# DeltaNet followed by a hardswish MLP on one core: the triangular problems stored with rows and columns changed over, and the first steps in another order

## The chip, the cores and the metric

The kernel runs on one core of one Trainium2 chip. A core has five engines with a queue of instructions each: TensorE (PE, with its weight loads shown as PEld), VectorE (DVE), ScalarE (ACT), GpSimd (POOL) and SyncE (SP), which here issues most of the DMAs. Each engine takes its instructions strictly in order; an instruction that waits holds up everything behind it on its engine. The metric is the device time of one execution in microseconds. A profiled execution has a span, from its first to its last instruction, and a time of its own, which is a little longer.

## The reference

Two blocks in a row. The first is a delta-rule attention over 768 steps, for 4 batches x 8 heads with heads of 48 elements; the second is an MLP on the 3072 x 384 result.

```python
k_n = k / (np.linalg.norm(k, axis=-1, keepdims=True) + 1e-06)
for t in range(S):                          # S = 768
    y[:, :, t] = einsum('bhd,bhde->bhe', q[:, :, t], state)
    v_old = einsum('bhde,bhd->bhe', state, kt)
    state += bt * einsum('bhd,bhe->bhde', kt, vt - v_old)
x = y.transpose(0, 2, 1, 3).reshape(B * S, H * D)   # 3072 x 384
h = x @ w_in                                        # 384 x 2048
g = h * clip(h + 3, 0, 6) / 6
out = g @ w_out                                     # 2048 x 384
```

q, k, v and beta arrive as float32, the two weight matrices as float64.

## The kernel before, in words

**Chunks.** The 768 steps are cut into 24 chunks of 32. Inside a chunk the recurrence is solved in closed form: with L, the strictly lower triangle of the chunk's scaled k-by-k products, one needs X, the inverse of a unit triangular 32x32 matrix, for each of the 32 pairs of batch and head. The partitions are 4 batches x 32 positions.

**The steps of one chunk t** (names as in the profile). `load_k`, `load_q`, `load_v` issue the DMAs (lines 140 to 175), four per chunk and tensor. `norms` makes 1/|k|: ACT squares (L386), DVE reduces (L392), ACT takes the root (L396), DVE two reciprocals and two small steps (L399 to L410). `mask` (L458) makes beta times the triangle on POOL, `prep` scales k (kb, L480, POOL), turns kb and q on PE (pt, L496), copies them to KQ on ACT (L504), multiplies them on PE (sc, L517) and masks the products on DVE into L (first output of L528) and LB (second). `scaled` (L468) makes beta times k. `chain` carries the state: PE multiplies state and KQ (ks, L776), DVE forms R (L789), PE X times R (pz, L797), ACT copies it to Z (L883), PE makes the update su (L894), which DVE takes from the state (L909); for the output ACT (L813) and DVE (L789) form y from ks, PE makes py (L797), DVE adds it (L832; for chunk 0 ACT copies it, L830), PE turns y (yt, L842) and ACT writes xT (L846).

**The inverses.** Chunk 0 is group 0, then there are six groups of up to four chunks. For chunk 0 `product` builds X out of 32x32 products on PE (pi, L566) with copies and transposes between them (L574 to L626, V by ACT in L594 and L613). For every other group the 128 problems of four chunks are laid on the 128 partitions: `taken` (L448) moves all of L into the tile A by one DVE transpose of 32x32 blocks, so that one partition holds one whole 32x32 matrix; a column-by-column elimination follows, two DVE instructions for each column (L700 and L705 in `halves_of`, L729 and L734 in `inverse`), then a memset of the diagonal (L710, L738), and `given` (L452) moves the result back into X. Group 1 goes by `halves_of`, which solves the two 16x16 halves of every matrix, and `join` (pi, L654, with L661 to L680) puts the halves together chunk by chunk; the others go by `inverse`.

**Weights.** The float64 weights come in 16 pieces of 768 KB (`load_w`, L310). DVE and ACT put together their float32 values: ACT four scale steps for each piece (L335), DVE three (L357, L362, L368).

**The MLP.** `up` multiplies a piece of w_in with xT (ph, L948), ACT and DVE make the activation g (L956, L959), `down` multiplies by w_out (po, L988); from the third block of 256 tokens on, `down_by_seven` makes it from seven products of half size (po, L1053, with DVE sums L1039). Block 0 is made in two halves of 128 tokens, the words `ua` and `ub`.

**What sets the order.** The first part of the program, up to and including the MLP of block 0 and the second group's inverse, is written out in `ORDER`, a list of 804 words (lines 22 to 44). Each word takes one step of a generator: `k`, `q`, `v`, `B`, `w` issue one DMA (k, q, v, beta, weight piece); `z` are settings, one of which turns beta (L234); `s` are POOL's memsets; `n0` to `n9` norms; `m` mask, `p` prep, `b` scaled; `x0` the product for chunk 0, `x1` to `x4` the joins; `i1` and `i2` the inverses of groups 1 and 2; `h` chain, `y` output; `a` ACT's scale steps; `c` DVE's share of the weights; `ua`/`ra`/`ga`, `ub`/`rb`/`gb`, `u`/`ru`/`gu` the MLP's products and its two activation steps; `e` its outputs. The order of the words fixes each engine's queue. Behind `ORDER` a loop over the chunks (L1262) issues the rest in a fixed plan. SP's DMAs share eight completion semaphores with beta's, which ACT issues: each DMA waits for the one eight places before it.

The lines that hold the layout of A:

```python
def problems(A):                                          # L444
    return A.rearrange("p (c i) -> p i c", i=C)
def taken(g, A):
    nc.vector.transpose(out=problems(A), in_=turn(Ls[g]))
def given(g, A):
    nc.vector.transpose(out=turn(inverted(g)), in_=problems(A))
```

`turn` views L or X as 32 positions i times 32 chunk-and-head pairs, a step of 32 elements between neighbours of the innermost axis.

Of the kernel before, what the change touches and what calls it, by code (L numbers as in the profile page):

```python
# [15 lines left out]
ALU = mybir.AluOpType  # L16
# [6 lines left out]
k*3 B k B*3 z n0*3 w z*3 s z q*2 n0 q n0 q v n0 w n0 a p0 a p0 s p0*2 m0 k*2 w p0 a*3 p0 a c a c v  # L23
p0 x0 a c k a x0*4 k a k x0 c k w*2 n1 c a c*2 k a x0 a*2 k a x0 k c*2 x0*2 n1 v c n1 k a q n2 c w
x0 a x0*2 k*2 m1 a*3 n1 s n2 c n1 a*2 x0 n1 c k*2 x0 n1 v x0 b0 n2 p1 c a n2 s b1 q h0 a c*2 h0 c
n2 w n2 a m2 k h0 s n2 q c z k q p1 n4 a y0 a p1 n2*2 p2*2 h0 q a p1 s*2 q*2 n4 p3 w q c n4 p2 c
p1 n4*2 p3 c n4 q*2 n4 b2 c a p2 p3 q*2 p2 p1 a q p2 c q*2 a p2 k p3 a p3 p4*3 q k m3 p4*2 s p1 p3
v p4 c y0 w y0*2 p3 ua m4 p4 ra ua b4 ua i1*6 ra*2 i1 k w ga i1*2 a ga ua ra i1*2 ua ga*2 i1 ra q
ua v ra a ua v i1 ga i1 ra ga ua s q i1*2 ua i1 ga i1 ra*2 ga i1 a i1*3 h1 ua i1 ra ga v ua ra
i1*2 v a ga i1*2 ga ua ra i1*2 ua a ga y1 i1 ua i1 x1 w x2 ra ua x2 x1 x2 ra ga*2 a x1 ra x1 k x1  # L30
ua x3 k x3 c x1 ra h1 y1 c h1*2 v y1 ga y1*2 q x3 c*2 w x3 a*2 y1 ub a v ub c ga h1 c rb*2 ub q rb
x2*2 k gb*2 v h1 ub q gb ub*2 rb c h2 n5 gb rb h2 gb k x2 ub a m5 v rb gb rb ub c gb y2 ub h2 q rb
w ub gb rb v n5 y2 u gb ub x4 a h2 k*2 q rb q n5 k*2 a n5 a k c rb y2 h2 y2 k gb a k n5 a ub gb y2
h2 ub c rb gb h3 rb ub gb v y2 c k q n5 v x3 h3 x3 y3 k*2 w k h3 a h3 b3 n5 u y3 rb x4 y3 a k n5*2
a w gb y3 c ub k n5 y3*2 rb gb c v n5 c u n5 u h3 ru gu a ru n5 a gu p5 h3 n9 x4 v c p5 b5 u p5 u
a*2 q h4 a p6 p5 a p5 x4 u v ru k c u a ru gu y4 n9 b6 x4 m6 v c q h4 k q gu u x4 k y4 p6 p7 u q
k*3 p6 k p7 h4 k n9 a q h4 p8 p7 p5 a c p5 k u n9 k p7 ru gu h4 p6 p7 m7 n9 h4 q b7 q u a c p6 n9
u p8 ru gu u k c k v n9*2 p8 c n9 b8 n9*3 p6 p8 w u n9 p6 c p8 p7 p8 p7 p9 ru m8 u p8 gu u c q ru
# [9 lines left out]
def kernel(  # L48
# [22 lines left out]
    B, H, S, D = q.shape  # L71
    DM, FF = moe_w_in.shape
    C, DP = 32, 64
# [118 lines left out]
    for j, value in enumerate((1.0, -1.0)):  # L192
        m = mask2[:, j, :]
        for b in range(B):
            nc.gpsimd.memset(mask2[rows(b), j, :], value)
            nc.gpsimd.affine_select(
                out=mask2[rows(b), j, :], in_=mask2[rows(b), j, :], pattern=[[1, C]],
# [246 lines left out]
    def problems(A):  # L444
        return A.rearrange("p (c i) -> p i c", i=C)
# [888 lines left out]
```

## Time and profile before

| | |
|---|---|
| three runs | 691.79, 689.22, 691.63 us; median 691.63 |
| the profiled execution | 690.61 us, its span 688.9 us |
| PE busy | 644.7 us, 94% of the span |
| DVE, ACT, POOL busy | 464.3, 239.1, 92.9 us |
| chain that ended last | PE 76%, DVE 14%, DMA 4%, issue 2%, SP's queue 2% |
| L948 (ph) | 1248 records, 270.0 us |
| L448, L452 (the block transposes) | 6 and 6, 2104 and 2081 ns |
| L729, L734 (the elimination) | 150 and 150, 335 and 361 ns |
| L335 (ACT's scale steps) | 56, 940 ns |

Float32 matmuls appear as two records each, so 32 matmuls are 64 records. The granted clock (PEclk) is the share of its full speed that TensorE was allowed. An engine's idle time counts only where that engine, or one that waits for it, carries the end; a row's releaser is the last thing that the waiting instruction had to have.

### The profile page before, as it was taken

The page shows a single profiled execution, that of the slowest core. Times are in us where ns is not written, and L with a number is a line of the kernel's source. Part 1 is how long each engine was busy: PE and PEld are TensorE (multiplying, and loading weights), DVE is VectorE, ACT ScalarE, POOL GpSimd, SP SyncE. Part 2 cuts the span into 40 slices and gives each one's busy share as a digit, 9 for nine tenths or more (in the row PEclk, how much of TensorE's full clock was granted, in tenths as well). Part 3 has the DMA queues.
Part 4 walks back from the last instruction along what each step waited for, and adds up shares of the span by engine and source line. Part 5 has one row for each costly group of instructions (what it writes and reads, how often), then busy time and mean ns, then how long its engine had stood idle before and what let it go on. Part 6 is the DMA issues. An engine that isn't in the chain of part 4 may idle for free.

```text
span 688.9 us, 25309 instructions
## 1 busy us (share of the span) xinstructions
PE 644.7 (94%) x11208; PEld 565.0 (82%) x11208; DVE 464.3 (67%) x1210; ACT 239.1 (35%) x476; POOL 92.9 (13%) x147
## 2 busy tenths in 40 slices
PE   1468799999999999999999999999999999999997
PEld 1357687767678988988988988988988989989997
DVE  4798776799836986845986745985546985445242
ACT  4886378542132232232232232232232132132220
POOL 5063003331501100501100402100000000000000
PEclk9999799999999999999999999999999999999999
DMA  9877026402132030031020030020020020000000
GB/s 236 240 184 183 4 83 134 83 3 58 29 60 46 3 65 9 3 73 33 4 59 14 3 70 2 3 59 2 3 48 2 2 48 2 25 3 1 25 0 24
DMA packets 88494, 33.20 MB, mean 48 GB/s; under 512 B 80160, under 2 KB 83232, under 8 KB 88384
## 3 DMA queue, kind: packets, MB, share of 16 engines
q1 hardware_dynamic: 88128, 31.29, 19.9%
q8 instruction: 88, 1.44, 0.9%
q10 hardware_dynamic: 256, 0.30, 0.2%
q14 instruction: 22, 0.18, 0.1%
HBM read 26.84 MB, written 4.72 MB: 46 GB/s over the span
## 4 chain that ended last, share of the span: by engine, by line
PE 76%; DVE 14%; DMA 4%; issue 2%; SPq 2%; ACT 1%; POOL 0%; DVEq 0%; ACTq 0%
PE ph L948 33%; PE po L1053 21%; PE po L988 5%; PE ks L776 3%; PE pz L797 3%; DVE A L734 3%; PE pt L496 3%; PE su L894 2%; PE py L797 2%; DVE pr L729 2%; DVE g L1039 2%; PE sc L517 2%; DMA vf<-in_v_dram 1%; PE yt L842 1%; DVE R L789 1%
## 5 line engine op out<-in xcount | busy, mean ns | idle before, releaser
L948 PE MATMUL ph<-xT,w_in 128*128 128x256 f32 (+1 forms) x1248 | 270.0, 369 | 4.2 <-DVE g L959 2.9
L948 PEld LDWEIGHTS ph<-xT,w_in 128*128 128x128 f32 x1248 | 220.2, 192 | 33.9 <-DVE g L959 4.7
L956 ACT ACTIVATE g<-ph,halves 128x256 f32<-128x256 f32 (+1 forms) x208 | 94.8, 457 | 201.7 <-PE ph L948 200.9
L959 DVE SCALAR_TENSOR_TENSOR g<-g,ph 128x256 f32<-128x256 f32 (+1 forms) x208 | 81.0, 396 | 106.0 <-ACT g L956 105.8
L1053 PE MATMUL po<-w_out,g 128*128 128x192 f32 x640 | 113.3, 328 | 0.0
L1053 PEld LDWEIGHTS po<-w_out,g 128*128 128x128 f32 x640 | 103.8, 190 | 0.5
L1053 PE MATMUL po<-spare,g 128*128 128x192 f32 x480 | 84.8, 330 | 0.0
L1053 PEld LDWEIGHTS po<-spare,g 128*128 128x128 f32 x480 | 78.1, 190 | 1.8
L1039 DVE TENSOR_TENSOR g<-g 128x256 f32<-128x256 f32 x160 | 65.5, 463 | 0.5 <-PE po L1053 0.5
L734 DVE TENSOR_TENSOR A<-A,pr 128x30 f32<-128x30 f32 (+9 forms) x150 | 54.2, 361 | 3.7
L335 ACT ACTIVATE spare<-spare,places 128x768 uint16<-128x768 uint16 (+1 forms) x56 | 52.5, 940 | 4.1 <-DVE places L252 3.3
L729 DVE TENSOR_TENSOR pr<-A 128x30 f32<-128x30 f32 (+9 forms) x150 | 50.3, 335 | 3.0
L988 PE MATMUL po<-w_out,g 128*128 128x384 f32 x128 | 45.7, 493 | 0.0
L1060 ACT ACTIVATE o<-po 128x192 f32<-128x192 f32 x40 | 13.2, 330 | 88.1 <-PE po L1053 88.1
L480 POOL TENSOR_TENSOR kb<-kf,inv 128x384 f32<-128x384 f32 x24 | 21.6, 900 | 158.4 <-DVE inv L410 73.7
L458 POOL TENSOR_TENSOR mb<-beta_tok,mask 128x256 f32<-128x256 f32 x48 | 34.5, 741 | 47.2 <-DVE LB L528 47.1
L504 ACT ACTIVATE KQ<-pt 128x512 f32<-128x512 f32 x48 | 28.3, 595 | 35.0 <-PE pt L496 34.6
L846 ACT ACTIVATE xT<-yt 128x384 f32<-128x384 f32 x24 | 11.7, 487 | 64.3 <-PE yt L842 64.3
L988 PEld LDWEIGHTS po<-w_out,g 128*128 128x128 f32 x128 | 22.9, 190 | 11.9
L496 PE MATMUL pt<-ident,kb 128*128 128x128 f32 x96 | 16.2, 295 | 14.7 <-POOL kb L480 14.5
L909 DVE TENSOR_TENSOR state<-state,su 128x384 f32<-128x384 f32 x46 | 23.2, 546 | 9.7 <-PE su L894 9.7
L789 DVE SCALAR_TENSOR_TENSOR y<-ks,parity,y 128x192 f32<-128x192 f32 x46 | 17.0, 412 | 17.6 <-ACT y L813 17.6
(109 smaller groups left out, 601.3 us busy)
## 6 DMA issues: line engine op xcount, KB each, us to landing
kf<-in_k_dram SPq DMA_DIRECT2D x96, 48.0 KB, 2.5
qb<-in_q_dram SPq DMA_DIRECT2D x96, 48.0 KB, 2.3
vf<-in_v_dram SPq DMA_DIRECT2D x96, 48.0 KB, 2.1
out_dram<-o SPq DMA_DIRECT2D x92, 48.0 KB, 1.6
spare<-in_moe_w_in_dram SPq DMA_DIRECT2D x4, 768.0 KB, 5.9
w_out<-in_moe_w_in_dram SPq DMA_DIRECT2D x4, 768.0 KB, 5.8
w_out<-in_moe_w_out_dram SPq DMA_DIRECT2D x4, 768.0 KB, 5.8
spare<-in_moe_w_out_dram SPq DMA_DIRECT2D x4, 768.0 KB, 4.6
```

Of the source, the lines that this page charges most:

```text
L335: nc.scalar.activation(out=z, in_=z if n else d.bitcast(I16)[:, :, :, 3], func=func, bias=places[:, n : n + 1], scale=scale,)
L458: nc.gpsimd.tensor_tensor(out=mb[:, e], in0=beta_tok[:, t, e:H:2].unsqueeze(2).unsqueeze(3).to_broadcast([P, NP, 2, C]), in1=mask2[:].unsq ...
L496: nc.tensor.transpose(pt[:, p, :], src[:, 2 * p : 2 * p + 2].rearrange("p e w -> p (e w)"), ident[:])
L729: nc.vector.tensor_tensor(out=pv, in0=A[:, j, j + 1 :].unsqueeze(1).to_broadcast([n, j, w]), in1=A[:, 0:j, j].unsqueeze(2).to_broadcast([n ...
L734: nc.vector.tensor_tensor(out=A[:, 0:j, j + 1 :], in0=A[:, 0:j, j + 1 :], in1=pv, op=ALU.subtract)
L797: nc.tensor.matmul(ps[rows(place(b)), D * h : D * h + D], lhsT=m(h)[rows(b)], rhs=z[rows(b), D * h : D * h + D], start=True, stop=True, sk ...
L948: nc.tensor.matmul(ph[:, cols], lhsT=w_in[:, s, f * 128 : (f + 1) * 128], rhs=xT[:, s, cols], start=(s == 0), stop=(s == NKT - 1),)
L956: nc.scalar.activation(out=g, in_=ph, func=ACTF.Relu, bias=half, scale=1.0 / 6.0)
L959: nc.vector.scalar_tensor_tensor(out=g, in0=g, scalar=1.0, in1=ph, op0=ALU.min, op1=ALU.mult)
L988: nc.tensor.matmul(pos[c][:], lhsT=gs[blk, f // 2][:, f % 2, c * P : (c + 1) * P], rhs=w_out[:, f, :], start=(f == 0), stop=(f == NFC - 1),)
L1039: nc.vector.tensor_tensor(out=A(f, *out), in0=A(f, *a), in1=A(f, *b), op=op)
L1053: nc.tensor.matmul(ps[n][:], lhsT=A(f - f % 2, *a)[:, f % 2], rhs=b[:, f], start=(f == 0), stop=(f == HF - 1),)
```

## The change

A is stored as the transposed matrix: what was at place (c, i) is at (i, c). `problems` then is the tile in its plain order, the out side of L448 and the in side of L452 run without a step, and the elimination's products and subtractions take rows for columns, in `halves_of` and in `inverse`. The same numbers are computed by the same number of instructions of the same sizes.

`ORDER` is written anew. It holds the same 804 words, each as often as before, in another order. Its first line before and after:

```diff
-k*3 B k B*3 z n0*3 w z*3 s z q*2 n0 q n0 q v n0 w n0 a p0 a p0 s p0*2 m0 k*2 w p0 a*3 p0 a c a c v
+k z k*2 B*2 k B*2 z n0*3 z*2 n0 z m0 n0*3 w s z s a q*2 c a p0 m1 p0 k c k a q*2 p0 w p0 s p0 a*3
...
     def problems(A):
-        return A.rearrange("p (c i) -> p i c", i=C)
+        return A.rearrange("p (i c) -> p i c", c=C)
...
-        D2 = D2.rearrange("p k (c i) -> p k c i", i=C)
+        D2 = D2.rearrange("p k (i c) -> p k i c", c=C)
...
-            pv = pr[0:n, 0 : 2 * j * w].rearrange("p (k c i) -> p k c i", k=2, c=j)
+            pv = pr[0:n, 0 : 2 * j * w].rearrange("p (k i c) -> p k i c", k=2, c=j)
...
-                out=pv, in0=D2[:, :, j, j + 1 : HC].unsqueeze(2).to_broadcast([n, 2, j, w]),
-                in1=D2[:, :, 0:j, j].unsqueeze(3).to_broadcast([n, 2, j, w]), op=ALU.mult,
+                out=pv, in0=D2[:, :, j + 1 : HC, j].unsqueeze(3).to_broadcast([n, 2, w, j]),
+                in1=D2[:, :, j, 0:j].unsqueeze(2).to_broadcast([n, 2, w, j]), op=ALU.mult,
...
-                out=D2[:, :, 0:j, j + 1 : HC], in0=D2[:, :, 0:j, j + 1 : HC], in1=pv,
+                out=D2[:, :, j + 1 : HC, 0:j], in0=D2[:, :, j + 1 : HC, 0:j], in1=pv,
...
-                out=pv, in0=A[:, j, j + 1 :].unsqueeze(1).to_broadcast([n, j, w]),
-                in1=A[:, 0:j, j].unsqueeze(2).to_broadcast([n, j, w]), op=ALU.mult,
+                out=pv, in0=A[:, j + 1 :, j].unsqueeze(2).to_broadcast([n, w, j]),
+                in1=A[:, j, 0:j].unsqueeze(1).to_broadcast([n, w, j]), op=ALU.mult,
...
-                out=A[:, 0:j, j + 1 :], in0=A[:, 0:j, j + 1 :], in1=pv, op=ALU.subtract
+                out=A[:, j + 1 :, 0:j], in0=A[:, j + 1 :, 0:j], in1=pv, op=ALU.subtract
```

The queues that follow from the new words, for the first chunks. SP: the four pieces of the first k and the first weight piece as before, then half of the first q, half of the second k, the rest of q, the second weight piece, the rest of the second k. DVE: beta's transpose (L234) ahead of the first norm's reduction (L392) instead of behind it, the parity memsets (L255, L258) behind the first norm instead of behind six weight pieces. POOL: the first chunk's mask ahead of its kb. ACT: three scale steps before the first KQ and five after the second, then L594, instead of two and seven. PE: the second chunk's kb and q are turned among and behind the first chunk's products; ahead of the first join stand 24 matmuls ph, ks and 15 ph instead of 27, ks and 18; then the joins follow singly, and in chunk 1's chain su stands ahead of py and yt instead of behind them. From about 170 us of the profiled execution to the end PE, and DVE from the second group's L452 on, have the same queue in both.

## The prediction

> **What bounds the kernel now.** I read the page first: how busy each engine is, and where.
>
> ```profile
> PE 644.7 (94%) x11208; PEld 565.0 (82%) x11208; DVE 464.3 (67%) x1210; ACT 239.1 (35%) x476; POOL 92.9 (13%) x147
> ...
> PE   1468799999999999999999999999999999999997
> PEclk9999799999999999999999999999999999999999
> ```
>
> TensorE (PE) is the bound from about 85 us to the end; the missing tenths stand in the first five of 40 slices. Next I asked for the busy times by stage: stage, its length, then busy time of PE, PEld, DVE, ACT, POOL, the granted clock and the DMA share.
>
> ```profile
> 20.00:30.00 10.00, 4.08 (x192) 3.63 (x192) 8.33 (x14) 8.40 (x13) 0.00 (x0) 1.00 0.91 226
> 30.00:40.00 10.00, 5.76 (x254) 5.07 (x256) 8.08 (x17) 9.74 (x15) 4.67 (x8) 1.00 0.70 150
> 40.00:50.00 10.00, 7.31 (x239) 5.83 (x227) 9.61 (x29) 9.25 (x15) 4.18 (x6) 1.00 0.74 204
> ...
> 70.00:80.00 10.00, 6.80 (x321) 5.83 (x313) 6.00 (x15) 3.00 (x6) 0.00 (x0) 0.66 0.02 5
> ...
> 120.00:130.00 10.00, 10.00 (x230) 7.80 (x230) 7.05 (x17) 6.96 (x14) 3.59 (x5) 1.00 0.43 96
> ...
> 200.00:240.00 40.00, 40.00 (x754) 36.08 (x753) 29.12 (x76) 12.43 (x27) 6.13 (x8) 1.00 0.19 35
> ```
>
> Up to 50 us ACT is nearly full and PE waits; from 200 us PE has 40.0 of 40.0 us. From the moment at which PE is full, the rest is a fixed quantity of matmul work, and both versions issue that work in the same order. So what the head (0 to 55 us) and the join of the first group (55 to 110 us) save, the end receives whole, and nothing else can give much. Third, the instructions of PE and DVE in order of time (start, length, what, idle before it and who ended it):
>
> ```profile
> 55.19 2.94 PE L948 MATMUL ph<-xT,w_in 128*128 128x128 f32 x24 [0.58 <-ACT xT L846]
> 69.54 1.39 PE L654 MATMUL pi<-X,VY 16*32 16x16 f32 x128 [1.85 <-DVE VY L664]
> 74.06 1.65 PE L948 MATMUL ph<-xT,w_in 128*128 128x128 f32 x6
> 92.37 0.94 PE L948 MATMUL ph<-xT,w_in 128*128 128x128 f32 x6
> ```
>
> ```profile
> 8.49 0.98 DVE L234 STREAM_TRANSPOSE beta_tok<-spare 128x768 f32<-128x768 f32 x1 [2.02 <-DMA qb<-in_q_dram]
> 9.39 0.33 DVE L237 TENSOR_REDUCE eye<-ident 128x32 f32<-128x128 f32 x1
> 9.86 0.25 DVE L245 TENSOR_REDUCE corner<-ident 128x16 f32<-128x64 f32 x1
> 54.95 2.10 DVE L448 STREAM_TRANSPOSE A<-L 128x1024 f32<-128x1024 f32 x1
> 66.92 2.09 DVE L452 STREAM_TRANSPOSE X<-A 128x1024 f32<-128x1024 f32 x1
> ```
>
> The MLP's first matmuls (ph) start at 55.19, behind xT. The first group's inverse starts its transpose at 54.95 and frees the join's matmuls (pi) at 69.54. The same six ph records take 1.65 us at 74 us and 0.94 at 92: the granted clock is 0.66 in that stage, 0.50 between 72 and 76.
>
> The sum is made against the profiled execution: 690.61 us, a span of 688.9 and 1.71 around it. It lies 1.02 below the median of the three runs, 691.63.
>
> **Part 1, the layout.** Each group makes one transpose into A (L448) and one out of it (L452), 12 in all at 2.10 and 2.08 us. Before, A is stepped by 32 elements in both, and so are L and X; after, the A side runs without a step and the L or X side still steps. A transpose without any step costs 0.98 us for 768 elements and 0.446 for 256: 0.53 us per 512 elements, so 0.98 + 0.27 = 1.25 us for 1024. Each changed transpose therefore lies between 1.25 and 2.1. Which side is dear? Two reductions read with a step of 32: 64 elements take 0.25 us (L245), 128 take 0.33 (L237), 1.25 ns an element against 1.04 without a step, so a stepped read is nearly free and the stepped write must make the 2.1. L448 then goes to 1.25 and L452 stays: 6 x 0.85 = 5.1 us of DVE time. I take that; the ends are 0 and 12 x 0.85 = 10.2. The products and subtractions between them (L700, L705, L729, L734) change rows for columns. They already run every shape from few long rows to many short ones, and 198 elements cost 0.37 us as 9 rows of 22 and 0.36 as 22 rows of 9: zero, and this is the row itself, not cover.
>
> On the path lies only the first group's pair (54.95 and 66.92, both in the chain) and a little of the second's (139.34): **-0.85**, ends 0 and -1.7, and **-0.3** for the second, ends 0 and -1.3 (all PE idle time from 140 to 180 us is 0.58 + 0.76). The later groups are hidden by PE at 40.0 of 40.0.
>
> The Trainium skill's page "SBUF — State Buffer", section Specifications, says that every access which crosses to a new 16-byte line pays. By that a stepped read pays too and both transposes could stay near 2.1; the first group's term would be 0 and the forecast 0.85 higher. The two reductions speak against it.
>
> **Part 2, the first weight piece.** Its DMA stands fifth on SP's queue in both versions, behind the four pieces of the first k, and waits for nothing in both; the four beta DMAs go by ACT's queue. Zero. What does move on SP: two of the second chunk's k pieces go ahead of half of q, v's first piece goes back behind the next chunks' k, and the second weight piece waits for the first to land (8.61 instead of 6.20 us). Each SP DMA waits for the one eight before it, so I walked the issue times: pieces 2 to 8 go out at about 8.6, 10.5, 12, 16.5, 17.6, 26.5 and 27.5, against 6.2, 9.5, 12.5, 13, 18.4, 23.9 and 30.3. With 5.8 to 5.9 us to land, all are there before ACT comes to them (third piece: lands by about 17, read at 19.8).
>
> **Part 3, the order of the first steps.** DVE now transposes beta (8.49 to 9.47) before it reduces the first k norm (was 5.92), so root, two reciprocals and kb move back by 0.5 us; POOL makes the first mask ahead of kb, which DVE then doesn't wait for. From there ACT is the queue to follow. Before, ACT runs seven scale steps (L335, 0.945 us each) between the second KQ and the copy of the first product (L594, at 21.00); after, five, so L594 comes at about 19.5 and the second product starts at 20.4 instead of 21.90. Following ACT's new queue with the old durations, from the end of its second KQ: 29 scale steps 27.4, 4 squares 1.64, 3 roots 0.75, 8 KQ 4.0, two V copies 0.6, Z and y 0.9: 35.3 us. That begins at about 14.8 and ends with y at 50.1, against 53.40. Before, the same walk has 36.2 us of work from 14.57 and 2.6 us of waits (1.50 at 28.74 for DVE, 0.60, 0.86, 0.26). In the new queue the tight places have slack: V's second copy 0.65 us, the second root 0.8, Z about 0. The last sc waits for the last KQ (49.7), yt ends near 51.2, ph starts near 51.7: -3.5. If the new order has 2.6 us of waits too, it is -0.9. I take **-3.0**, nearer the walk, for Z's missing slack. PE does the same matmuls up to there in both, so this is a plain shift.
>
> In the join PE gets 13 column blocks of ph (0.73 us each) ahead of its first pi instead of 15, then only the first chunk's pi, its pz, and su ahead of py. Counted from the start of ph, the inverse takes as long as before (28 steps and 10 instead of 11 g). PE's idle times before, in order: 0.65, 1.85, 0.93, 0.98, 0.61, 0.68, 0.58, 0.58 = 6.9 us. After, with old transposes: 0.8 where ph waits for g (DVE takes the third g after seven pairs, not five), 2.6 until the first pi, 0.9 until the second, 0.6 for R (queued behind L357 on DVE), 0.6 for Z, 0.6 for y, 0.7 for the next pz, 0.58 twice: 8.0. So +1.1. Against it stands the slow clock: two ph (1.65 and 1.49 against 0.94), pz (1.50 against 0.88), pi (1.29 against 0.73) and su (1.20 against 0.89) lost 2.7 us before; with state updated some 14 us sooner and ph work left to fill in, I take that half of it stays: -1.35. Ends: +1.1 and -1.6; sum **-0.25**. The moved parity memsets (0.44 us of DVE) go into DVE's wait for sc (3.19 us before), zero; without that wait they would cost their 0.44.
>
> The page "TensorE: Matmul & The Clock Gate", section "What's actually happening", has the half clock after an idle window of about 3.4 us. Here 0.50 followed 68 to 72 us, in which PE was busy 1.5 of 4 us, with no single gap above 1.85. By the page alone my gaps of at most 2.6 us would leave the clock full and the sum 1.35 lower; the row says that a sparse stretch is enough.
>
> **Sum.** -0.85 - 0.3 - 3.0 - 0.25 = -4.4 on 690.61: 686.2. Half of the distance to the median added: **686.7 us**.
>
> **Rivals.** (a) The transposes stay at 2.1, the step on either side being enough: L452 at 2.08 against L448 at 2.10 doesn't tell the sides apart. -3.25: 687.9. (b) The head's gain is eaten: ACT keeps its 2.6 us of waits (-0.9) and the join costs +1.1 at the old clock, -0.85 and -0.3 remain: about -1, 690.2. For it speaks that ACT's slack is under 1 us at four places. (c) Slower: the join is sparse enough to hold the clock at half for long. At half clock 1.65 us do the work of 0.94, so 10 us of it lose 4.3; before it held for some 9 us between 70 and 84. To turn the forecast's -4.4 into +3.5 takes 7.9 us, 18 further microseconds of it; 25 give +10.8 - 4.4 and 697. Against it: after 85 us PE has no gap above 0.58, and the clock came back within 4 us of dense ph work.
>
> **Numbers.** What a measurement of this kernel tells from no change is 0.5%, 3.5 us: faster is below 688.2, slower above 695.1. Forecast 0.53, of which 0.50 faster and 0.03 same; (a) 0.15, at the border, 0.09 faster and 0.06 same; (b) 0.18, same; (c) 0.14, slower. So 0.59, 0.27 and 0.14. Low end: -3.5 - 1.7 - 1.3 - 1.6 = -8.1 with a run as fast as the profiled one, 682. High end: (b) and the milder half of (c), 694.5. The forecast's own range is 684 to 689.
>
> **What would show it.** Right: L448 near 1.25 and L452 near 2.08; L594 near 19.5; y near 50; the first ph near 51.7; state's second update near 71 instead of 84; PE idle from 55 on about 7 us. Wrong: an ACT wait of more than 1 us between 15 and 50 (a weight piece or a product late); L448 still 2.1; a granted clock below 0.7 for more than 10 us after 60; or PE idle time after 140 us, which would mean that DVE, not PE, had become the bound.

## The result, and the profile after

The changed kernel takes 693.45 us (median of 20 executions, 690.22 to 696.64); before takes 691.32 us (20 executions, 689.22 to 695.41). The ratio is 1.0028, with a 95% interval of 1.0010 to 1.0045: slower by some 2 us, within the 0.5% that the forecast called the same, and 6.8 us above the forecast of 686.7. In a second set of runs the ratio was 1.0033 (1.0014 to 1.0051).

The profiled execution after took 690.50 us with a span of 688.8, next to 690.61 and 688.9 before. It is one of the quickest of the 20, so it flatters the change by about 3 us; the medians carry the verdict, the profile shows the places.

First the page of the changed kernel: the busy times, PE in 40 slices, and the granted clock.

```profile
PE 646.2 (94%) x11208; PEld 567.6 (82%) x11208; DVE 465.5 (68%) x1210; ACT 239.6 (35%) x476; POOL 96.1 (14%) x147
...
PE   1677899999899999999999999999999999999997
...
PEclk9989899999999999999999999999999999999999
```

The second and third slice of PE have risen from 4 and 6 to 6 and 7; the fourth has fallen from 8 to 7. And PE is 1.5 us longer busy with the same matmuls, and the clock has a dip in the third slice that before had not. The same stages as in the prediction (stage, its length, busy times of PE, PEld, DVE, ACT, POOL, granted clock, DMA share, GB/s):

```profile
20.00:30.00 10.00, 5.80 (x256) 5.39 (x256) 8.89 (x19) 9.84 (x14) 0.91 (x1) 1.00 0.87 215
30.00:40.00 10.00, 6.22 (x227) 4.83 (x222) 9.45 (x19) 9.84 (x16) 4.43 (x6) 0.97 0.87 209
40.00:50.00 10.00, 8.27 (x252) 7.26 (x252) 8.67 (x15) 8.97 (x14) 6.83 (x9) 0.69 0.77 189
70.00:80.00 10.00, 8.17 (x317) 7.24 (x313) 6.04 (x14) 5.37 (x9) 0.00 (x0) 0.66 0.13 23
...
200.00:240.00 40.00, 40.00 (x753) 36.08 (x752) 29.12 (x76) 12.45 (x27) 6.15 (x8) 1.00 0.20 36
```

ACT is fuller up to 40 us (9.84 of 10 against 8.40 and 9.74): the new order does pack it. From 200 us on nothing has changed. Now PE in order of time (start, length, what, idle before it and who ended it), first before and then after; the counts are of records, two to a matmul:

```profile
37.26 1.17 PE L797 MATMUL pz<-vf,X 32*32 32x48 f32 x44 [0.98 <-issue]
...
47.39 0.99 PE L517 MATMUL sc<-KQ 64*32 64x64 f32 x68 [0.64 <-issue]
...
180.27 0.86 PE L517 MATMUL sc<-KQ 64*32 64x64 f32 x64 [1.03 <-ACT y L813]
```

```profile
37.65 0.35 PE L797 MATMUL py<-Z,LB 32*32 32x48 f32 x10
39.90 1.33 PE L797 MATMUL py<-Z,LB 32*32 32x48 f32 x54 [1.90 <-issue]
...
48.04 0.71 PE L517 MATMUL sc<-KQ 64*32 64x64 f32 x46 [0.47 <-ACT KQ L504]
50.49 1.04 PE L517 MATMUL sc<-KQ 64*32 64x64 f32 x82 [1.74 <-issue]
...
52.59 2.94 PE L948 MATMUL ph<-xT,w_in 128*128 128x128 f32 x24 [0.58 <-ACT xT L846]
...
66.06 0.73 PE L654 MATMUL pi<-X,VY 16*32 16x16 f32 x64 [1.19 <-DVE VY L664]
...
180.39 0.86 PE L517 MATMUL sc<-KQ 64*32 64x64 f32 x64 [1.78 <-ACT y L813]
```

The first ph starts 2.6 us sooner than before, at 52.59. The first two lines to look at are those that end in "issue": in the middle of a run of equal small matmuls, after the 10th py and after the 46th sc, PE stands still for 1.90 and 1.74 us and waits for no engine and no data that the profile shows. Before has two such pauses ahead of ph, of 0.98 and 0.64 us. The last sc stands straight ahead of yt and ph. What fed it was early, as ACT's line for y shows. Below it are DVE's block transposes of the first group and of the second:

```profile
19.18 0.36 ACT L594 ACTIVATE VY<-pi 128x256 f32<-128x256 f32 x1
...
48.84 0.50 ACT L830 ACTIVATE y<-py 128x384 f32<-128x384 f32 x1
```

```profile
8.29 0.98 DVE L234 STREAM_TRANSPOSE beta_tok<-spare 128x768 f32<-128x768 f32 x1 [6.24 <-DMA qb<-in_q_dram]
...
52.35 1.97 DVE L448 STREAM_TRANSPOSE A<-L 128x1024 f32<-128x1024 f32 x1
63.57 1.96 DVE L452 STREAM_TRANSPOSE X<-A 128x1024 f32<-128x1024 f32 x1
...
137.61 1.98 DVE L448 STREAM_TRANSPOSE A<-L 128x1024 f32<-128x1024 f32 x1
170.68 1.95 DVE L452 STREAM_TRANSPOSE X<-A 128x1024 f32<-128x1024 f32 x1
```

The second group's pair before:

```profile
139.34 2.12 DVE L448 STREAM_TRANSPOSE A<-L 128x1024 f32<-128x1024 f32 x1
170.41 2.07 DVE L452 STREAM_TRANSPOSE X<-A 128x1024 f32<-128x1024 f32 x1
```

y starts 4.1 us sooner than before (52.92), ph only 2.6. And the transposes cost 1.97 and 1.96 us: the layout has brought 0.13 us each, not 0.85.

Where do the 2.6 us go? PE's idle time from the first ph to the ks of chunk 5 (at about 171 us) is 8.55 us against 7.57, summed over the stages between; its busy time for nearly the same work is 0.9 longer; some 0.8 us of lead are left at 171, and between 177 and 181 us, where PE waits for y (1.78 us against 1.03), they go too. From there to the end the two profiles run 0.1 us apart. DVE's rows tell where y is held up: the second group's transpose into A starts 1.7 us sooner than before (137.61 against 139.34), the one out of it 0.3 later (170.68 against 170.41). Two microseconds of lead are lost between the two.

### The profile page after: what moved, and what is told of

It is laid out like the page before. It is cut to its first block, busy times and chain, and to the rows that moved or that the text cites. A ratio compares the mean times of both kernels' runs of the same rounds, so it can differ in the third digit from the quotient of the medians.

```text
span 688.8 us, 25313 instructions
## 1 busy us (share of the span) xinstructions
PE 646.2 (94%) x11208; PEld 567.6 (82%) x11208; DVE 465.5 (68%) x1210; ACT 239.6 (35%) x476; POOL 96.1 (14%) x147
## 3 DMA queue, kind: packets, MB, share of 16 engines
q8 instruction: 88, 1.44, 0.9%
## 4 chain that ended last, share of the span: by engine, by line
PE 73%; DVE 14%; DMA 4%; issue 4%; ACT 3%; SPq 1%; POOL 0%; DVEq 0%; POOLq 0%; ACTq 0%
PE ph L948 33%; PE po L1053 21%; PE po L988 4%; PE py L797 3%; PE ks L776 3%; DVE A L734 3%; PE pz L797 2%; DVE pr L729 2%; PE su L894 2%; DVE g L1039 2%; PE sc L517 2%; PE pt L496 2%; ACT spare L335 2%; DMA kf<-in_k_dram 1%; DVE R L789 1%
## 5 line engine op out<-in xcount | busy, mean ns | idle before, releaser
L734 DVE TENSOR_TENSOR A<-A,pr 128x30 f32<-128x30 f32 (+9 forms) x150 | 54.6, 364 | 3.6
L729 DVE TENSOR_TENSOR pr<-A 128x30 f32<-128x30 f32 (+9 forms) x150 | 50.5, 337 | 3.0
L480 POOL TENSOR_TENSOR kb<-kf,inv 128x384 f32<-128x384 f32 x24 | 23.0, 965 | 156.0 <-issue 69.7
L776 PEld LDWEIGHTS ks<-state,KQ 64*64 64x64 f32 x1472 | 23.8, 134 | 7.7 <-issue 6.9
```

Of the source, the lines that this page charges most:

```text
L729: nc.vector.tensor_tensor(out=pv, in0=A[:, j + 1 :, j].unsqueeze(2).to_broadcast([n, w, j]), in1=A[:, j, 0:j].unsqueeze(1).to_broadcast([n ...
L734: nc.vector.tensor_tensor(out=A[:, j + 1 :, 0:j], in0=A[:, j + 1 :, 0:j], in1=pv, op=ALU.subtract)
L776: nc.tensor.matmul(ph[y][c, e, D * p : D * p + D], lhsT=KQ[r, p * B // 2 + b // 2, 2 * y : 2 * y + 2, :].rearrange("k y c -> k (y c)"), rh ...
```

## Experiments

Medians are in us; ratios are to the runs of before on the same chip, with their 95% intervals. "New head" is the first 225 words of `ORDER` as changed (to the first matmul of ph), "new rest" all that follows; where a head and a rest of different origin are joined, the rest's words keep their order and those that the head has already taken are left out.

### Which part of the change costs: the layout or the order

```diff
 e1:  problems(), halves_of(), inverse() as changed; ORDER as before
 e2:  ORDER as changed; problems(), halves_of(), inverse() as before
 e3:  the changed kernel
```

> The new layout with the old order of the steps. Theory: the layout is worth almost nothing and costs nothing. A transpose falls from 2.10 to 1.97 us, about 0.13 us each, two of them on the path of the first group: 691 us, ratio to before 0.998 to 1.001, granted clock as before (0.990). Rival (the layout is what costs, since rows and columns of the elimination steps are changed over): ratio 1.002 to 1.004, and the elimination steps L729 and L734 dearer than 335 and 361 ns.

> The new order of the steps with the old layout. Theory: the order makes the whole of the result. It starts ph some 2.5 us sooner, and gives that back in the join, to half-clock stretches and at the second group's inverse on DVE: ratio to before 1.002 to 1.005, a granted clock about 0.003 to 0.01 below that of before. Rival (the layout costs): ratio 0.996 to 1.000.

> The changed kernel once more, to learn whether the difference of the medians (693.45 against 691.32 us) comes again, and to have a second profile of it. Theory: it comes again, ratio 1.001 to 1.005, and the executions that take longer show a lower granted clock: about 3 us for each 0.01. Rival (chance): ratio 0.999 to 1.001.

| kernel | median | ratio |
|---|---|---|
| e1 layout alone | 690.88 | 0.9996 (0.9982 to 1.0011) |
| e2 order alone | 692.56 | 1.0032 (1.0013 to 1.0051) |
| e3 changed kernel | 693.27 | 1.0033 (1.0014 to 1.0051) |

The layout does nothing that can be measured, for or against; the elimination steps L729 and L734 cost 336 and 362 ns against 335 and 361. The order makes the whole difference. The guess in e3's expectation, about 3 us for each 0.01 of the granted clock, didn't hold: over e3's 12 executions the correlation is -0.16, and over the executions of all kernels, each taken against the mean of its own kernel, 0.01 goes with 1.0 us (correlation -0.36). The order does lower the clock, from a median of 0.990 (before, e1) to between 0.982 and 0.984 (after, e2, e3); by that slope an estimate of 0.7 us of the 2.

### What a step costs in the block transpose

```diff
-nc.vector.transpose(out=problems(A), in_=turn(Ls[g]))
+nc.vector.transpose(out=A.rearrange("p (i c) -> p i c", c=C), in_=Ls[g][:].rearrange("p t h i -> p (t h) i"))
 (and the same on both sides of the transpose out of A)
```

> The changed kernel with no step on either side of the block transposes, L448 and L452, so that blocks are not regrouped (this leaves out the right placement of the problems and their inverses). If one stepped side is enough for the dear price, both rows fall to about 1.25 us (the estimate from 0.98 us for 768 and 0.446 for 256 elements). If 1024 elements cost about 2 us whatever the step, both stay at 1.96. Time: with 2 x 0.7 us less before the first join and 2 x 0.7 us less in the second group's inverse, 1 to 2 us less than the changed kernel, if DVE sets the pace there.

The two groups of the transposes, by line (count, busy, mean ns, idle before; the second has moved to L455):

```profile
L455 DVE STREAM_TRANSPOSE X<-A 128x1024 f32<-128x1024 f32 x6 | 7.5, 1244 | 0.2
L448 DVE STREAM_TRANSPOSE A<-L 128x1024 f32<-128x1024 f32 x6 | 7.4, 1236 | 0.0
```

So 1.24 us without any step (the estimate of 1.25 was right), 1.96 to 1.97 with a step on either side, 2.08 to 2.10 with both. Either side alone brings nearly the whole price. The Trainium skill, "SBUF — State Buffer", section Specifications, has each cross to a new 16-byte line pay a penalty. That a step on either side costs agrees with it; that the second side adds only 0.12 us is more than it says. The time of the one execution, 692.3 us, doesn't show the 1 to 2 us that was expected; it lies within the spread of the changed kernel.

### Which part of the order costs: the head or the rest

```diff
 e5:  ORDER = new head + old rest   (new layout)
 e6:  ORDER = old head + new rest   (new layout)
```

> The new layout; the first 225 steps in the new order (up to the first matmul of ph), all that follows in the order of before. Theory: the head's gain of 2 to 3 us at the first ph is real, and the end does not get it because the new order puts 2.0 us more DVE work between the two block transposes of the second group (33.07 us against 31.08), on the path. With the old order there the stretch is 31.1 us again and the end receives most of the head's gain: ratio to before 0.996 to 0.999. Rival (the half-clock stretches of the join take the gain, whatever order follows): ratio 1.000 to 1.003 with the stretch at 31.1 us.

> The new layout; the first 225 steps in the order of before, all that follows in the new order. Theory: no gain at the first ph (54 to 55 us), the second group's stretch on DVE 33.1 us: ratio to before 1.003 to 1.007. Rival (the head itself costs, by half-clock stretches that it makes): ratio 1.000 to 1.001.

e5: 692.78, ratio 1.0016 (0.9996 to 1.0036). e6: 693.27, ratio 1.0032 (1.0012 to 1.0051). Against e1 that is +1.4 us for a head that was to bring 3, and +2.5 us for the rest, each give or take 1.7. The theory failed for e5, although the second group's stretch on DVE was 31.06 us as it said: the head's gain was not there to be received. The ratio lies in the range of the rival (half-clock stretches in the join), but ph itself was late. The profile of e5 shows why, in PE's order of time:

```profile
48.45 0.71 PE L517 MATMUL sc<-KQ 64*32 64x64 f32 x46 [0.91 <-ACT KQ L504]
52.20 1.44 PE L517 MATMUL sc<-KQ 64*32 64x64 f32 x82 [3.04 <-issue]
...
55.05 1.22 PE L948 MATMUL ph<-xT,w_in 128*128 128x128 f32 x4 [0.58 <-ACT xT L846]
```

After the 46th sc again, now for 3.04 us, and ph starts at 55.05 as it did before the change.

### Is it the second group's inverse on DVE

In the profiles DVE takes 33.07 us from L448 to L452 of the second group with the new rest and 31.07 with the old one, because the new order puts, among others, a reduction, two reciprocals and two small steps of later norms there. From 140 to 170 us DVE is busy 27.99 of 30 us in both. Three runs on whether that is the loss:

```diff
 e7:  ORDER: the last seven words n9 (and four words k that they need) ahead of the first i2
 e8:  inverse(2):  if 12 <= j < 20: yield; yield; continue
 e16: inverse(2), old order:  taken(g, flat) twice
```

> The changed kernel, with the last seven norm steps of the fourth group (one reduction, two reciprocals, two small steps on DVE: 1.22 us) taken out of the second group's inverse and put ahead of it, as before has them; one k piece goes out earlier for it. Theory: the stretch between L448 and L452 of the second group falls from 33.1 to about 31.5 us and the time by 1 to 1.6 us against the changed kernel: ratio to before 1.000 to 1.002. Rival (the stretch is not on the path): no change, 1.003. If L448 begins as much later as the stretch is shorter, also no change.

> The changed kernel without 8 of the 30 elimination pairs of the second group (columns 12 to 19, about 0.83 us a pair, 6.6 us of DVE; that part of the inverse is left out). If DVE's second-group inverse sets the pace, the time falls until PE is the bound again: PE's idle time between 164 and 185 us is 2.2 us, so 2 to 3 us less than the changed kernel, ratio to before 0.998 to 1.000, and L452 comes 6 us sooner. If the end hangs on PE's work alone, it stays at 1.003.

> The new layout with the old order, and the second group's transpose into A (L448) made twice: 1.97 us more DVE work at the start of the second group's inverse, as much as the new order puts there. Theory (that stretch sets the end, so that the new order loses 2.0 us there): ks of the sixth chunk 2 us later and ratio to before 1.002 to 1.003. Rival (there is slack, and the new order's rest loses by something else): 0.9996, as without.

| kernel | median | ratio |
|---|---|---|
| e7 norms ahead | 696.42 | 1.0077 (1.0052 to 1.0101) |
| e8 eight pairs less | 690.70 | 0.9988 (0.9968 to 1.0008) |
| e16 transpose twice, old order | 691.08 | 0.9996 (0.9981 to 1.0011) |

e7 missed: L448 began at 139.30 instead of 137.61 and the stretch grew to 33.78 us, with waits of DVE for ACT (1.62 us) and for PE (0.59) in it that had not been there. e8 took the time that was expected of it, 3.1 us less than the changed kernel (give or take 1.9), but not by L452 coming 6 us sooner: 6.6 us less of DVE work made the stretch only 1.5 us shorter (31.54), since DVE then waits 3.45 us for the activation behind PE. e16's median shows no price of 1.97 us more DVE work (0.0 us against e1, give or take 1.4). In its profile

```profile
141.45 3.98 DVE L448 STREAM_TRANSPOSE A<-L 128x1024 f32<-128x1024 f32 x2
```

the two transposes take 4.0 us, but L452 follows at 173.34, so the stretch is 31.89: it took up about a microsecond of the 1.97 and is longer by 0.8. A price of 0.8 us is too small for the medians.

The traces of all the runs tell more than these three medians. From each, the start of the second group's L448, that of its L452, and the end of the span:

| profiles | L448 to L452, us | L448 to the end, us |
|---|---|---|
| old rest: before, e1, e5, e11, e12, e15, e17, e18 | 31.06 to 31.08 | 549.2 to 549.6 |
| old rest, transpose twice: e16 | 31.89 | 550.2 |
| new rest: after, e3, e6, e9, e13 | 33.05 to 33.08 | 551.2 to 551.6 |
| new rest, 3.4 us at half clock from 184 us on: e2, e14 | 33.09, 33.07 | 553.1, 552.5 |
| the same, with other changes: e7, e10 | 33.78, 33.49 | 553.7, 553.6 |
| new rest, transposes without a step: e4 | 33.08 | 550.8 |
| new rest, eight pairs less: e8 | 31.55 | 550.1 |

Whatever stands in front, the end follows the start of this inverse at a fixed distance: 2.0 us more with the new rest, 0.8 more in e16, about 1.3 less in e8 than in the five of the new rest. The rows say how. In DVE's queue L452 stands ahead of the next norms' reductions (L392), ACT's root waits for these, y stands behind the root on ACT, and PE's sc waits for y: it starts 9.7 to 9.9 us after L452 in nineteen profiles (9.1 in e4, whose L452 is 0.7 us shorter). So every profile of the new rest with the whole inverse pays 2.0 us or more here, and a lead that PE has ahead of 180 us is waited away at y. Four of the eleven profiles of the new rest (e2, e7, e10, e14) also have 3.4 us of half clock from about 184 us on, by these distances an estimate of 1.2 to 1.9 us each; none of the nine of the old rest has. On the way there the rests hardly differ: from the first ph to L448 it is 86.5 us on average with the old one and 86.4 with the new one, each with a scatter of 6 us. The theory of the 2.0 us thus stands for the rest, which costs 2.5 us by e6, though no run took just these steps out; it explains nothing of the head.

### Is it the half clock

```diff
+def dense(ps, n):
+    for _ in range(n):
+        nc.tensor.matmul(ps[:, 0:128], lhsT=ident[:], rhs=ident[:], start=True, stop=True, ...)
 e10 (changed kernel): 8 ahead of the first chunk's pi1 and pi2, 9 ahead of the next pz
 e11 (new layout, old order): 14 ahead of pi1, 7 ahead of pi2
```

> The changed kernel with filler for PE where it waits in the join: 8 matmuls of 128x128x128 without use before each of the first chunk's two pi, 9 before the next chunk's pz, about 1 us at each place, where PE waits 1.19, 1.05 and 1.26 us. If the half-clock stretches between 65 and 95 us come from PE's idle windows there and cost time, the stretches shrink (5.1 to 20 us in the six profiles so far) and the time falls 1 to 4 us against the changed kernel: ratio to before 0.998 to 1.002. If they don't hang on PE's idle time, or the filler stands in the way, 1.003 to 1.006.

> The new layout with the old order, and the same filler: 14 matmuls before the first pi (PE waits 1.72 to 1.85 us there) and 7 before the second (0.93 to 0.95 us). If idle windows make the half-clock stretch of 6.8 us that both profiles of the old order have at 70 us, it goes, and with it up to 3.4 us: ratio to before 0.995 to 0.999. If not, 1.000 to 1.003.

e10: 693.79, ratio 1.0050 (1.0030 to 1.0071). e11: 693.37, ratio 1.0037 (1.0019 to 1.0055). In e11 the 14 stand behind chunk 2's pi1, which comes ahead of chunk 1's, so that PE's wait of 1.72 us in front of both is still there. The filler did keep the clock: e10's profile has no half stretch between 44 and 105 us, and e11's has none at all but for the last 3 us,

```profile
core 0: 689.2 us, clock 1.000
```

and over e11's eight executions its median is 0.998, where e1 has 0.990. The time still rose, by 2.8 us from e1's ratio to e11's. The filler isn't free: the 42 records at pi1 and pi2 take 5.2 us and replace 2.5 us of waits. So the half clock is worth something (in e11's profile the state's update of the second chunk starts 0.9 us sooner than in e1's in spite of the filler), but not what the filler costs. As a cause of the difference between the orders it is not excluded by these two runs; the estimate above leaves it 0.7 us, the stretch at 184 us included.

### Is it PE's supply of instructions

The pauses come after the same record in every profile of the new head with all its loads (10th py: 1.65 to 3.77 us; 46th sc: 0.72 to 3.04 us). The page lists a DMA queue of 88 packets for instructions:

```profile
q8 instruction: 88, 1.44, 0.9%
```

1.44 MB over 11208 matmul records and as many weight loads is 64 bytes each, so one packet of 16 KB feeds 128 records with their weight loads. Between the 10th py and the 46th sc lie 252: two packets. The places are those of the packets and not of either order: counted along PE's queue, the pauses stand behind record 476, 728 and 1235 before the change and behind 602, 854 and 1236 after it, and all 70 pauses of 0.25 us or more between 15 and 250 us in the twenty profiles lie within two records of one grid with steps of 126 to 129. By the trace's DMA records, packets ended at 38.72 and 48.78 us in the changed kernel, and the pauses at 39.90 and 50.49. In all 70 the last packet to end before PE goes on is the one due at that place (the fourth of the trace at record 602, the sixth at 854), and PE goes on 1.2 to 1.8 us after its end. Three weight pieces of 768 KB were issued at 43.67, 46.67 and 48.82 us, just there; before issues them at 38.5, 40.6 and 48.2. Hence four runs with less to load; they leave out seven eighths of the pieces named:

```diff
+rs = slice(0, 16 if 6 <= i <= 10 else P)          # e13: 8 <= i <= 10
 nc.sync.dma_start(out=raws[i].rearrange("p s f z -> p s (f z)")[rs], in_=src.bitcast(U32)[rs])
 e9, e13: changed kernel   e12: new layout, old order   e17: new layout, new head, old rest
```

> The changed kernel with weight pieces seven to eleven cut to 16 of 128 partitions, an eighth of their bytes (the rest of those weights is left out). In every profile of the new head, PE pauses without a wait inside two runs of small matmuls: before py (1.65 to 3.77 us, near 38 us) and before the last sc (0.90 to 3.04 us, near 49 us), and a fetch of instructions by DMA ends 1.2 to 1.7 us before each pause does, while three pieces of 768 KB were issued between 43.7 and 48.8 us. Theory (the fetch stands behind the weight pieces): both pauses fall below 1 us, ph starts at 50 to 51.5 us, and of that the end gets 0 to 2 us. Rival (PE outruns its fetch whatever else is loaded): pauses of 0.9 to 3 us as before and ph at 52 to 55 us.

> The control to the cut of the weight pieces: the new layout with the old order, the same pieces seven to eleven cut to 16 of 128 partitions (the rest of those weights is left out). In the new order the cut took the time from 1.003 to 0.9954 of before. Theory (the new order is the one that puts fetches of instructions behind weight pieces; the old order pauses only 0.7 to 1.6 us in the head): the old order gains less, 1 to 2.5 us, ratio 0.996 to 0.9985. Rival (less DMA traffic is worth the same in any order, so that it doesn't tell why the new order lost): ratio 0.992 to 0.993, as far below the old order (0.9996) as the new one fell.

> The changed kernel with only weight pieces nine to eleven cut to an eighth (the rest of those is left out); seven and eight come whole. These three were issued between 43.7 and 48.8 us, just ahead of the pause before the last sc; seven and eight stand ahead of the pause before py. Theory: the pause before the last sc goes (below 0.7 us), that before py stays (1.6 us or more), ph starts at 51 to 52.5 us and the time lies between the changed kernel and the larger cut: ratio 0.997 to 1.000. If the pause before py is the dear one, 1.001 to 1.003.

> The new head with the order of before behind it, the new layout, and weight pieces seven to eleven cut to an eighth (the rest of those is left out). Theory: no pause for instructions before the last sc, ph at 50 to 51.5 us, and no 2.0 us on DVE behind it: 1 to 2 us below the same cut in the changed kernel (0.9954), ratio 0.992 to 0.995. Rival (the old rest takes the head's gain too, as it took the 1.3 us by which the first ph of the layout alone came sooner than before's): 0.996 to 0.999.

| order | all loads | pieces seven to eleven cut |
|---|---|---|
| old head, old rest | 0.9996 (e1) | 0.9991 (0.9977 to 1.0005), 690.28 us (e12) |
| new head, old rest | 1.0016 (e5) | 0.9943 (0.9926 to 0.9959), 687.55 us (e17) |
| new head, new rest | 1.0033 (e3) | 0.9954 (0.9935 to 0.9974), 687.11 us (e9) |

This is the answer for the head. The cut is worth 0.3 us to the old order and 5.0 and 5.5 us to the new head, whichever rest follows. Without the pauses the head brings what it was meant to: e17 lies 0.0048 below e12, 3.3 us (give or take 1.5), and in their profiles the first ph starts at 50.66 against 53.89. PE in e9 and then in e17:

```profile
38.61 1.33 PE L798 MATMUL py<-Z,LB 32*32 32x48 f32 x54 [0.63 <-issue]
...
47.64 1.71 PE L518 MATMUL sc<-KQ 64*32 64x64 f32 x128
50.41 2.95 PE L949 MATMUL ph<-xT,w_in 128*128 128x128 f32 x24 [0.58 <-ACT xT L847]
```

```profile
38.13 1.87 PE L798 MATMUL py<-Z,LB 32*32 32x48 f32 x64
...
47.77 1.83 PE L518 MATMUL sc<-KQ 64*32 64x64 f32 x128 [0.48 <-ACT KQ L505]
50.66 2.94 PE L949 MATMUL ph<-xT,w_in 128*128 128x128 f32 x24 [0.58 <-ACT xT L847]
```

The 128 sc now run without a break. e13 (691.99 us, ratio 1.0010, 0.9988 to 1.0031) cut the last three pieces alone:

```profile
41.67 1.34 PE L798 MATMUL py<-Z,LB 32*32 32x48 f32 x54 [3.02 <-issue]
...
49.78 1.83 PE L518 MATMUL sc<-KQ 64*32 64x64 f32 x128 [0.92 <-ACT KQ L505]
52.67 2.94 PE L949 MATMUL ph<-xT,w_in 128*128 128x128 f32 x24 [0.58 <-ACT xT L847]
```

The pause before the last sc is gone, the one in py stays, as was expected for each, and ph starts at 52.67; the time lies at the lower end of the range that was named for the case that the pause before py is the dear one. The pause in py hangs on pieces seven and eight (issued at 29.63 and 30.65 us; 23.9 and 30.3 before): cutting these two as well is worth 3.9 us (e9 against e13), cutting the last three 1.6 (e13 against e3), each give or take 2.

The traces show the load on the packets themselves. From the time at which PE passes the place of the packet before, the fourth packet takes 3.8 to 6.0 us to its end in the eight profiles of the new head with all loads, and 1.9 and 2.3 in e9 and e17; the sixth takes 3.4 to 5.4, and 2.4 and 3.0. In e13 the fourth still takes 5.4, the sixth 2.7. So the late packets are where the pauses are, and they are late while the pieces are under way. No run delayed the packets by themselves; that a part of the 5 us came by another way that less load opens is not excluded.

The first ph, in all profiles: with all loads where they were, 53.72 to 55.19 for the old head (five profiles, mean 54.3) and 51.93 to 55.23 for the new one (eight, mean 53.5); with the cut 53.89 and 50.4 to 50.7. The new head gains 0.7 us on average, and 3.4 where the loads are out of the way.

### Can the gain be had with all the loads

```diff
 e14: changed kernel; word of the ninth piece 32 words sooner;
+     eng = nc.scalar if i in (9, 10) else nc.sync        # tenth and eleventh piece, behind xT
 e15: the same with new head and old rest
 e18: as e15, with the tenth to thirteenth piece by ACT's queue, spread over 55 to 76 us
```

> The changed kernel with all its loads whole: the ninth weight piece is issued 3 to 4 us sooner on SP's queue, the tenth and eleventh by ACT's queue behind xT (from about 52 us), so that none is under way while PE fetches the instructions of the last sc. Theory: the pause before the last sc falls below 1 us, ph at 51 to 52.5 us, the time 1 to 3 us below the changed kernel: ratio 0.998 to 1.001. Rival (the pieces then collide with something else, or the fetch is late anyway): 1.002 to 1.005.

> The same move of the weight pieces with the new head and the order of before behind it (and the new layout): the second group's stretch on DVE is 31.1 instead of 33.1 us. Theory: the gain of the head (ph at 51 to 52.5 us) meets no 2.0 us on DVE behind it: ratio 0.994 to 0.998, faster than both kernels. Rival: as the new head without the move, 1.000 to 1.003.

> An attempt at a faster whole kernel: the new head with the order of before behind it, the new layout, all loads whole; the ninth weight piece sooner on SP's queue, the tenth to thirteenth by ACT's queue at about 55, 58, 72 and 76 us, so that the stretch from 64 to 71 us, in which PE fetches for the join's matmuls, is free of them. Theory: the pause of 2.35 us in the first pi falls to about 1, ratio to before 0.996 to 0.999. Rival: it moves to another run of small matmuls, or ACT waits for a piece: 1.000 to 1.003.

| kernel | median | ratio |
|---|---|---|
| e14 | 695.02 | 1.0066 (1.0043 to 1.0089) |
| e15 | 690.31 | 0.9999 (0.9984 to 1.0013) |
| e18 | 692.25 | 1.0012 (0.9995 to 1.0029) |

In none of the three does the last sc lose more than 0.71 us to such a pause, and ph starts at 52.6 to 52.8. The pause in py, which hangs on the two pieces that none of the three moves, is still there (2.85, 3.30 and 2.48 us). And the pieces then stand in the way elsewhere. In e14 the twelfth and thirteenth piece moved back as well, to 68.55 us, and the DMA windows and PE's next py show it:

```profile
70.00:74.00 4.00, 3.39 (x149) 2.89 (x151) 2.34 (x5) 2.46 (x5) 0.00 (x0) 0.50 0.92 366
74.00:78.00 4.00, 1.06 (x53) 0.87 (x47) 1.06 (x3) 0.51 (x1) 0.00 (x0) 0.50 0.75 132
```

```profile
77.25 1.17 PE L798 MATMUL py<-Z,LB 32*32 32x48 f32 x43 [2.94 <-issue]
```

2.94 us, with the DMA engines at 0.92 and 366 GB/s ahead of it. In e15 the join's second pi pauses 2.35 us at 71.8, and in e18 there are pauses of 0.91 and 0.71 in two runs of sc, 1.14 in pi, 0.93 in ks and 1.60 in pz. None is faster than before. No run found a whole kernel that beats both.

## Why the prediction was wrong, step by step

**What head and join "save, the end receives whole".** This sentence failed twice. With the loads cut and the old rest behind it the end did receive the head's gain: 3.3 us for a head that was to bring 3.0 (e17 against e12). With the real loads it received nothing (e5), because the head itself was held up before its last step. And with the new rest it can't receive it whole: the prediction took PE for the bound from 85 us on, but from the second group's L448 to y at 180 us DVE carries the end, and the new order puts 2.0 us more there (33.07 against 31.07 us). The sum has no term for that. The prediction had named the sign, PE's idle time after 140 us: it is 2.2 us up to 200 us against 1.6 before. Of before's wait for y, 1.03 us, it had counted the 0.76 us up to the end of its window at 180, and then said that after 85 us PE has no gap above 0.58.

**Part 2 and the moved DMAs: zero.** This is the term that was wrong by the most. The walk through SP's queue was near enough (pieces two to four at 8.40, 10.34 and 11.86 us against 8.6, 10.5 and 12; five and six between 18.4 and 21.1, seven and eight at 29.63 and 30.65, some 2 to 3 us later than said), and all came before ACT needed them. But each transfer was held only against its own reader. What it delays meanwhile, the packets that bring PE its instructions, wasn't asked for, although before already shows three pauses marked "issue" (0.98, 0.64 and 0.98 us). The measured price is 5 us under the new head (e5 against e17), 0.3 under the old one.

**Part 3, the head: -3.0.** ACT's walk held: L594 at 19.18 (said: 19.5), y ending at 49.34 (50.1), and no wait of ACT above 0.28 us between 15 and 50. The sentence that failed is "PE does the same matmuls up to there in both, so this is a plain shift". The same matmuls closer together use up their instructions faster: the pauses ahead of ph were 3.64 us instead of 1.62 in the two profiles, and ph came at 52.59, on average of eight profiles at 53.5, instead of 51.7.

**Part 3, the join: -0.25.** PE's idle time up to the ks of chunk 5 rose by 1.0 us, as the +1.1 said. The other half, that the half clock would fall by half (-1.35), did not come: by the trace's clock records 10.2 us between 60 and 100 us run at half in both profiles, and the new order adds a stretch of 6.8 us at 39 that before doesn't have (before has 3.4 us at 50). The stretch that the prediction dates after 68 to 72 us began at 70.47, behind 3.41 us in which PE was busy 46%. With the old head in front (e6) the new rest cost 2.5 us (give or take 1.7). By the traces 2.0 of it lie in the second inverse, and the half clock at 184 us adds 1.2 to 1.9 in four of eleven profiles. With the loads cut the two rests differ by 0.0011, 0.8 us (e9, e17, give or take 1.8), which agrees with 2.0 and with nothing.

**Part 1, the layout: -0.85 and -0.3.** The transposes went from 2.10 to 1.97 us, so -0.13 each, and 0.3 us at most in the sum; rival (a), with 2.1, had the durations nearly right. The inference from the two reductions was wrong: they show that a reduction reads with a step for nearly nothing, and were taken as the nearest row for another operation. e4 shows that a step on either side of the block transpose costs 0.7 us, the second one 0.1. That the elimination steps cost nothing was right.

**The rivals.** (b), 690.2, named the outcome best, a head whose gain is eaten and a join at +1.1, but by ACT's waits, which did not come. (c), the half clock for long in the join, did not come: 10.2 us of it between 60 and 100 us in both profiles. Holding the clock at full with filler made nothing faster (e10, e11), but the filler has its own price; what is left to the clock is the 0.7 us estimated above.

The sum, from the profiles: the first ph 0.7 us sooner, the way from it to the second group's L448 0.1 shorter, 2.0 more from there on, and 0.6 more as the average of the half clock at 184 us: +1.8, against 2.0 measured. The agreement is better than the terms, since the first ph alone scatters over 3 us; by the medians the head is +1.4 and the rest +2.5, with intervals over 3 us wide.

## What to carry to other kernels

When an order is changed, charge every moved transfer with what it delays besides its own reader; here a run of many small matmuls got its instructions by DMA, and big loads under way just then stopped PE without any wait that names a cause. A pause marked "issue" at a fixed place inside equal instructions is that sign, and it grew when the run was packed tighter. Ask of every stage, too, which engine's rows the end follows: a full PE at 200 us doesn't make PE the bound at 150. A distance that is the same in every trace, as from the second inverse to the end, answers that better than the medians of runs that differ by a microsecond. And a control is worth its run: cutting the loads under the old order as well is what told a cause from a mere gain.

## What the runs showed of the hardware

- 16 KB of instructions are 128 small matmul records with their weight loads, and 128 of them take 1.5 to 2.1 us; the packets took 0.9 to 1.9 us each, with 1.2 to 1.8 us from a late one's end to PE's going on. With 768 KB pieces under way the fourth and the sixth packet of the new head ended 3.4 to 6.0 us after PE had passed the place of the one before, without them 1.9 to 3.0. PE stood still for up to 3.8 us.
- A block transpose of 128x1024 f32 on DVE: 1.24 us without a step, 1.97 with a step of 32 elements on one side, 2.10 on both.
- The clock halves in stretches that are multiples of 3.41 us. In the twenty profiles, 42 such stretches began between 15 and 110 us, each behind a window of 3.41 us in which PE was busy 19 to 69%; others as sparse were followed by none (before, 20 to 30 us: busy 4.08 of 10 us at a granted clock of 1.00). The Trainium skill, "TensorE: Matmul & The Clock Gate", section What's actually happening, has the half clock follow an idle window of about 3.4 us: the length agrees, but these windows were far from idle.
- In e3's profile the clock was at half from 18.7 to 46 us, and ph still started at 51.93, the earliest of the new heads with all loads: where PE waits for others anyway, the half clock cost little.
